# Attention of the first four tiles in the form of the later ones, with a set time for each step of the plan

## The chip, the cores and the metric

One core of a Trainium2 chip runs the whole program. The time is device microseconds of one execution, given as the median of three runs; the profile is of a fourth execution, taken by the hardware profiler, with its own time. The engines are TensorE (PE; its weight loads PEld), VectorE (DVE), ScalarE (ACT), GpSimd (POOL) and SyncE (SP), which issues all the transfers of this kernel on one queue.

## The reference

Chunked attention, then two pairs of dense layers on its output:

```python
# q, k, v: (4, 8, 768, 64); mem_k, mem_v: (4, 8, 8, 64); chunks of 32, 16 to the left, 8 to the right
for c in range(nc):
    q_c = q[:, :, c_start:c_end]
    k_full = np.concatenate([mem_k, k[:, :, l_start:r_end]], axis=2)
    v_full = np.concatenate([mem_v, v[:, :, l_start:r_end]], axis=2)
    scores = scale * np.matmul(q_c, k_full.transpose(0, 1, 3, 2))
    scores = scores - np.max(scores, axis=-1, keepdims=True)
    a = np.exp(scores)
    a = a / (np.sum(a, axis=-1, keepdims=True) + 1e-09)
    out[:, :, c_start:c_end] = np.matmul(a, v_full)
x = out as (3072, 512)
h = x @ w_in;  g = np.maximum(h, 0) + alpha * np.minimum(h, 0);  x = g @ w_out        # 512 -> 2048 -> 512
h = x @ w2_in; g = h * np.tanh(softplus(h));                     out = g @ w2_out
```

The weights come as 64-bit floats.

## The kernel before

The 3072 rows are 24 tiles of 128 rows (T); four tiles make a block of 512 rows. Each number is split into a high and a low part (`xh`, `xl`; `gh`, `gl`), and a product is three matmuls. The program is in stages: the attention of tiles 0 to 3; layer 1 over the blocks, into which the attention of the later tiles is woven two tiles at a time; the last blocks of layer 1 and then layer 2 in a form with seven products for eight.

Nothing runs in the order in which it is written. Every operation is given to a plan (`plan.add`) with an engine, an estimated duration and what it reads and writes. `Plan.run` derives due times backwards from the TensorE operations, whose own due time is `plan.now` at the moment of adding (a running sum of TensorE durations), plays the plan through with these estimates, and emits each engine's operations in the order that comes out. Before the first matmul of layer 1 the gaps that the plan sees on TensorE are filled with matmuls on a zero tile (`busy`).

Three kinds of steps make the attention of a tile: scores `s`, transposes `t` and values `v`; `first` lists them for the tiles 0 to 3. There are two forms:

- **The first four tiles** (`scores_of`, `turn_pe`, `values_of`). The queries of two heads lie in one wide tile (`qbd`) whose other halves GpSimd sets to zero and into which VectorE (ScalarE once) copies the loaded rows (`place`); a score matmul gives 64 x 64. The probabilities lie in wide rows padded with zeros, and 16 small transposes a tile turn them; the values lie on 96 partitions, and a value matmul contracts over these.
- **The later tiles** (`scores_late`, `turn_late`, `values_late`), two at a time. The queries are used as they are loaded, a score matmul gives 32 x 64 in one of two banks, one 128 x 128 transpose serves two heads, and the values lie on 2 x 64 partitions, so that a row needed by two chunks is loaded twice.

For the tiles in `WHOLE` (2 and 3) the exponential is one instruction after a subtraction on VectorE, with a sum behind it; for the others it is one instruction for each of eight groups, which gives the sum too.

A `gate` is a transfer of one element out of a tile. It can only be issued when the tile has landed (or been scaled by ScalarE), and it holds the queue until then, so that the loads behind it start later:

```python
add("sp", 0.001, lambda: nc.sync.dma_start(gated[:, n : n + 1], first() if first else b.t[0:1, 0:1]), [b], at=-1.0, not_before=when)
```

A weight is loaded as 64-bit words (`load_raw`, L320 for input weights, L325 for output weights), scaled by ScalarE (L339), put together by VectorE (L342, L345) and split (L356, L359). `evac` stores the output of layer 1 in `yd`; `reload1` loads a split output weight back (`wo<-w1o`, L418); `sent` loads a weight of layer 2 (`wo<-w2i`, L437).

Lines: scores L632, exponentials L650 (by group) and L660 (whole), transposes L868 and copies out of them L267, values L699, layer 1's first product L1087 and second L1136, rectifier L1106 and L1107, fillers L1684. In the later form: scores L755, transposes L892, values L821 and their loads L591 and L598.

Of the kernel before, what the change touches and what calls it, by code (L numbers as in the profile page):

```python
# [20 lines left out]
NEG = -1.0e30  # L21
# [169 lines left out]
def chunked_attention_moe_moe_kernel(  # L191
# [39 lines left out]
    WHOLE = (2, 3)  # L231
# [37 lines left out]
    def dma_(b):  # L269
        return max(0.45, b / (285e3 if not plan.now else 310e3 if 390 < plan.now < 700 else 265e3))  # L270
# [173 lines left out]
    spare = [(side, j) for j in range(NJ - 1, NJ - 7, -1) for side in "oi"]  # L444
# [10 lines left out]
    qbd = [own([P, 1024], f"qbd{i}") for i in range(2)] + [spare_slot() for _ in range(2, T0)]  # L455


    q_own, upper = ([Buf(lambda b=b, lo=lo: b.t[:, lo : lo + 512], [b]) for b in qbd[:2]] for lo in (0, 512))
    kring = ring(ac, [P, NP * KC], F32, "kt", 1)
    vring = ring(ac, [P, 2 * DM], F32, "vw", 1)  # L460
    q_rows = [spare_slot() for _ in range(T0 // 2)]
# [3 lines left out]
    s_bufs = [own([P, 1024], "s"), spare_slot()]  # L465
    a_bufs = [own([P, 1024], "aT"), spare_slot()]

    def wide_of(b):
        return b.t.rearrange("p (g w) -> p g w", w=P)

    for b in s_bufs:
        for cols in (slice(0, CH), slice(CH + SW, P)):
            add("pool", 0.6, lambda b=b, cols=cols: nc.gpsimd.memset(wide_of(b)[:, :, cols], 0.0), writes=[b])
    for b in qbd:
        for h in range(2):
            add(
                "pool", 0.6,
                lambda b=b, h=h: nc.gpsimd.memset(
                    b.t.rearrange("p (g h x) -> p g h x", g=2 * NP, h=2)[(1 - h) * 64 : (2 - h) * 64, :, h], 0.0
                ),  # L480
                writes=[(b, 2 + h)],
            )
    stats = ring(ac, [P, 3, 2 * NP], F32, "st", 3)
    stats2 = ring(ac, [P, 3, 4 * NP], F32, "su", 2)
# [3 lines left out]
    att_bufs = [*s_bufs[:1], *a_bufs[:1], *qbd[:2], *q_own, *upper]  # L488
    n_ps = [0]
# [16 lines left out]
    def load_qk(T):  # L506
        b, t = divmod(T, TPB)
        if T >= T0:
            load_qk_late(T)
            return  # L510
        kt = kv_spare[T][0] if T in kv_spare else kring.next()
        qt = qbd[T]

        def kview():
            return kt.t[:, : NP * KC].rearrange("p (a c) -> p a c", a=NP)

        def qview():
            return qt.t.rearrange("p (a e h x) -> p a e h x", a=NP, e=2, h=2)

        add("sp", dma_(P * NP * KC * 4), lambda: nc.sync.dma_start(kview(), kw[b, t]), writes=[kt])  # L520
        if T == 3:
            gate(kt, 12.7)

        row = q_rows[T // 2], T % 2

        def rows():
            return row[0].t[:, row[1] * 512 : (row[1] + 1) * 512]

        add("sp", dma_(P * 2048), lambda: nc.sync.dma_start(rows(), q[b, t].rearrange("h d a e x -> (h d) (a e x)")), writes=[row])
# [7 lines left out]
        kts[T], qs[T] = (kt, kview), (qt, qview)  # L537
        att_bufs.append(kt)

# [30 lines left out]
    def load_v(T):  # L570
        b, t = divmod(T, TPB)
        if T < T0:
            v = kv_spare[T][1] if T in kv_spare else vring.next()
# [5 lines left out]
            vws[T] = v, lambda: v.t[:W].rearrange("w (e h d) -> w e h d", e=2, h=H)  # L579
            att_bufs.append(v)  # L580
            return

        bufs = upper if T % 2 else [vring.next()]
        for e in range(2):
            half = slice(e * 64, (e + 1) * 64)
            rows = vw[b, 2 * t + e].rearrange("w h d -> w (h d)")
            if T % 2:
# [13 lines left out]
        if not T % 2:  # L601
            att_bufs.append(bufs[0])

        def value(half, c, h):
            x = (0 if T % 2 else c * DM) + h * D
            return bufs[c if T % 2 else 0].t[half, x : x + D]
# [3 lines left out]
    def scores_of(T):  # L610

        t = T % TPB
        (kt, kview), (qt, qview) = kts[T], qs[T]
        bk = att_bank(T, 6)
        sb = s_bufs[T % 2 if T < T0 else 0]

        def s():
            return wide_of(sb)[:, :, CH : CH + SW]

        st = stats.next()  # L620
        ss[T] = sb

        def ps():
            return bk.t.rearrange("p (g c) -> p g c", c=SW)


        def go():
            for e in range(2):
# [11 lines left out]
        def clip():  # L640
            if t == 0:
                nc.vector.memset(ps()[0:64, 0:NP, 0:16], NEG)
# [1257 lines left out]
```

## Time and profile before

| | |
|---|---|
| median of 3 runs | 1056.91 us (1055.81 to 1058.74) |
| the profiled execution | 1057.76 us, span 1056.0 us |
| TensorE busy | 1048.8 us (99%) |
| VectorE, ScalarE busy | 766.8 us (73%), 603.4 us (57%) |
| granted TensorE clock | 1.000 |
| transfers | 256.68 MB, mean 243 GB/s |

The span is from the first to the last instruction; the time of an execution has a little more around it. A busy TensorE is one with a matmul in flight. Times of the trace are us from the start of the span.

### The profile page before, as it was taken

Reading aid. Unit: us, or ns where it says so; the run is one execution under the profiler, and the core shown is the slowest. Engines: PE = TensorE matmul, PEld = TensorE weight load, DVE = VectorE, ACT = ScalarE, POOL = GpSimd, SP = SyncE. Lnnn points to the kernel's source line nnn. Section 1 sums busy time; section 2 is a strip of 40 time slices with the busy share of each in tenths; the row PEclk is TensorE's granted clock in tenths of the full one; section 3 lists DMA queues with packets and bytes.
Section 4 is the critical chain, followed back from the end, with each engine's and each line's share of the span. In section 5 each row is a group of like instructions: output and inputs, shape, how many; then the busy total and the mean of one; then the engine's idle time right before and its main releaser. Section 6 shows DMA issues by size and latency. Waiting matters only on the chain.

```text
span 1056.0 us, 22372 instructions
## 1 busy us (share of the span) xinstructions
PE 1048.8 (99%) x8235; PEld 904.2 (86%) x8235; DVE 766.8 (73%) x1621; ACT 603.4 (57%) x1496; POOL 6.8 (1%) x19
## 2 busy tenths in 40 slices
PE   9999999999999999999999999999999999999998
PEld 6888888888888888888878889999999999999998
DVE  7999578878987899887792246875476875475586
ACT  6888555565667456666674344654454654454453
POOL 2000000000000000000000000000000000000000
PEclk9999999999999999999999999999999999999999
DMA  8978776785888764556789977787887778778786
GB/s 265 311 243 250 246 280 203 249 289 183 272 265 261 242 183 121 173 170 198 251 284 314 314 257 233 223 263 250 263 271 251 224 244 253 225 242 252 232 260 211
DMA packets 136742, 256.68 MB, mean 243 GB/s; under 512 B 13882, under 2 KB 38970, under 8 KB 136634
## 3 DMA queue, kind: packets, MB, share of 16 engines
q1 hardware_dynamic: 136634, 255.26, 75.0%
q8 instruction: 65, 1.06, 0.4%
q14 instruction: 43, 0.35, 0.1%
HBM read 203.56 MB, written 51.64 MB: 242 GB/s over the span
## 4 chain that ended last, share of the span: by engine, by line
PE 97%; DMA 1%; ACT 0%; SPq 0%; DVE 0%; issue 0%; DVEq 0%; ACTq 0%
PE bank L1377 23%; PE bank L1245 22%; PE bank L1136 17%; PE bank L1087 16%; PE bank L1666 8%; PE bank L1570 7%; PE bank L821 2%; PE bank L755 1%; PE bank L1684 1%; DMA wo<-w1o 1%; DMA wo<-in_w_out_dram 0%; PE bank L632 0%; SPq L437 0%; PE bank L699 0%; PE bank L892 0%
## 5 line engine op out<-in xcount | busy, mean ns | idle before, releaser
L1245 PE MATMUL bank<-wi,wo 128*128 128x512 f32 x672 | 180.8, 393 | 0.0
L1087 PE MATMUL bank<-xh,wi 128*128 128x512 f32 (+1 forms) x528 | 171.1, 386 | 0.2 <-ACT rstrip L1107 0.2
L1136 PE MATMUL bank<-gh,wo 128*128 128x512 f32 x512 | 169.6, 392 | 0.0
L1245 PEld LDWEIGHTS bank<-wi,wo 128*128 128x128 f32 x672 | 121.5, 189 | 21.2
L1087 PEld LDWEIGHTS bank<-xh,wi 128*128 128x128 f32 x528 | 98.1, 188 | 20.3 <-ACT rstrip L1107 0.4
L1136 PEld LDWEIGHTS bank<-gh,wo 128*128 128x128 f32 x512 | 96.2, 188 | 20.3
L1087 PE MATMUL bank<-xl,wi 128*128 128x512 f32 (+1 forms) x264 | 101.2, 384 | 0.0
L1136 PE MATMUL bank<-gl,wo 128*128 128x512 f32 x256 | 99.8, 390 | 0.0
L1245 PE MATMUL bank<-wo,wo 128*128 128x512 f32 x336 | 93.1, 393 | 0.0
L1377 PE MATMUL bank<-wo,wi 128*128 128x256 f32 x588 | 80.4, 283 | 0.0
L1377 PEld LDWEIGHTS bank<-wo,wi 128*128 128x128 f32 x588 | 77.1, 191 | 3.0
L1377 PE MATMUL bank<-wo,wo 128*128 128x256 f32 x558 | 76.9, 283 | 0.0
L1377 PEld LDWEIGHTS bank<-wo,wo 128*128 128x128 f32 x558 | 73.8, 191 | 3.1
L1099 ACT CAST gh<-rstrip 128x512 fp32r<-128x512 f32 x64 | 40.8, 638 | 54.3 <-DVE rstrip L1110 37.7
L1245 PEld LDWEIGHTS bank<-wo,wo 128*128 128x128 f32 x336 | 60.8, 189 | 10.1
L1110 DVE SCALAR_TENSOR_TENSOR rstrip<-rstrip,nalpha 128x512 f32<-128x512 f32 x64 | 47.9, 749 | 20.0 <-ACT rstrip L1107 19.1
L1106 ACT ACTIVATE rstrip<-bank 128x512 f32<-128x512 f32 x64 | 39.6, 619 | 33.9 <-PE bank L1087 33.7
L1087 PEld LDWEIGHTS bank<-xl,wi 128*128 128x128 f32 x264 | 49.7, 188 | 9.3
L909 DVE STREAM_TRANSPOSE aT<-s 32x256 f32<-32x256 f32 x128 | 55.8, 436 | 2.3
L1100 DVE TENSOR_TENSOR gl<-rstrip,gh 128x512 fp32r<-128x512 f32 x64 | 43.9, 687 | 18.1 <-ACT gh L1099 17.8
L1136 PEld LDWEIGHTS bank<-gl,wo 128*128 128x128 f32 x256 | 48.1, 188 | 9.8
L774 ACT ACTIVATE s<-bank,su 128x64 f32<-128x64 f32 x160 | 49.1, 357 | 4.4 <-DVE su L791 4.4
(416 smaller groups left out, 1994.7 us busy)
## 6 DMA issues: line engine op xcount, KB each, us to landing
wo<-w2o SPq DMA_DIRECT2D x237, 256.0 KB, 3.3
wo<-w2i SPq DMA_DIRECT2D x168, 256.0 KB, 3.4
wo<-w1o SPq DMA_DIRECT2D x49, 512.0 KB, 4.1
w2o<-wo SPq DMA_DIRECT2D x57, 256.0 KB, 3.0
w2i<-wo SPq DMA_DIRECT2D x56, 256.0 KB, 3.4
wo<-in_w_out_dram SPq DMA_DIRECT2D x24, 512.0 KB, 7.1
wi<-in_w_in_dram SPq DMA_DIRECT2D x16, 512.0 KB, 8.6
w1o<-wo SPq DMA_DIRECT2D x16, 512.0 KB, 5.3
```

The source lines that it names most:

```text
L774: nc.scalar.activation(s()[:, i, z, g], ps(z)[:, i, g], AF.Exp, bias=st.t[:, 0, n : n + 1], scale=0.125, accum_out=st.t[:, 1, n : n + 1],)
L909: nc.vector.transpose(dst[:, :, m // 2, m % 2], src[:, :, keys])
L1087: nc.tensor.matmul(bk.t[:, lo:hi], a, b, start=kk == 0 and i == 0, stop=kk == KT - 1 and i == 2)
L1099: add("act", a_(n), lambda: nc.scalar.copy(g.t[0], src.t[0]), [src], [(g, "h")], at=at)
L1100: add("dve", d_(n), lambda: nc.vector.tensor_sub(g.t[1], src.t[0], g.t[0].bitcast(F32)), [src, (g, "h")], [(g, "l")], at=at)
L1106: add("act", a_(n) - 0.05, lambda: nc.scalar.activation(m.t[0], h.t[:, :n], AF.Relu, scale=-1.0), [h], [m], at=at)
L1110: lambda: nc.vector.scalar_tensor_tensor(r.t[0], m.t[0], nalpha[:, j : j + 1], r.t[0], ALU.mult, ALU.add),
L1136: nc.tensor.matmul(bk.t[:, :n], lt, rh, start=j == 0 and i == 0, stop=j == NJ - 1 and i == 2)
L1245: nc.tensor.matmul(bk.t, l, r, start=start and kk == n == 0, stop=kk == 1 and n == 2, skip_group_check=True,)
L1377: nc.tensor.matmul(bk.t[:, s * HB : (s + 1) * HB], g.t[:, zg * HB + s * P : zg * HB + (s + 1) * P], piece()[:, zw * HB : (zw + 1) * HB], s ...
L1570: nc.tensor.matmul(bk.t, l, r, start=start and kk == n == 0, stop=kk == 1 and n == 2, skip_group_check=True,)
L1666: nc.tensor.matmul(bk.t, lt, rh, start=first and i == 0, stop=last_ and i == 2)
```

## The change

Tiles 0 to 3 use the form of the later tiles: `scores_of`, `values_of` and `turn_pe` are gone, and `scores`, `values` and `turn` (the former `_late` ones) work on one tile (`count(T)` is 1) or two. The queries are no longer copied and nothing is set to zero; each of the four tiles has its own `s` and `aT`. The values of a tile are two transfers to 64 partitions each. `WHOLE` holds tile 3 alone. The banks of the first tiles come from a list. The plan's clock is set by hand for each step of the first tiles and to 18.94 after them, where it was the sum of TensorE's durations. The estimate for a transfer and the gates' earliest times are changed.

```diff
-    WHOLE = (2, 3)
+    WHOLE = (3,)
 ...
-        return max(0.45, b / (285e3 if not plan.now else 310e3 if 390 < plan.now < 700 else 265e3))
+        return max(0.45, b / (345e3 if plan.now < 3 else 310e3 if 390 < plan.now < 700 else 265e3))
 ...
-    for b in qbd:
-        for h in range(2):
-            add(
-                "pool", 0.6,
-                lambda b=b, h=h: nc.gpsimd.memset(
 ...
+    n_ps = [-1]
+    FIRST = (0, 1, 2, 4, 5, 6, 7, 0, 1, 2, 4, 1, 7, 0, 1, 6, 1, 2, 6, 0)
 
     def att_bank(T, late):
         n_ps[0] += 1
-        return bank((0, 1, 2, 4, 5, 6, 7)[n_ps[0] % 7] if T < T0 else late)
+        return bank(FIRST[n_ps[0]] if T < T0 else late)
 ...
         if T == 3:
-            gate(kt, 12.7)
-
-        row = q_rows[T // 2], T % 2
 ...
-        for h in range(2):
-
-            def place(eng, h=h):
-                half = slice(h * 64, (h + 1) * 64)
-                copy_on(eng, qview()[half, :, :, h], rows()[half].rearrange("p (a e x) -> p a e x", a=NP, e=2))
-
-            add(BOTH if T == 0 else "dve", 0.55, place if T == 0 else partial(place, "dve"), [row], [(qt, h)])
+            gate(kt, 10.5)
 ...
-            src = vw[b, 2 * t : 2 * t + 2].rearrange("e w h d -> w e (h d)")
-            view = lambda: v.t[:W].rearrange("w (e x) -> w e x", e=2)
-            add("sp", dma_(P * 3520), lambda: nc.sync.dma_start(view(), src), writes=[v])
-            if T in (0, 2):
-                gate(v, 14.7 if T == 0 else 0.0)
 ...
+        apart = T >= T0 and T % 2
+        bufs = [kv_spare[T][1]] if T in kv_spare else upper if apart else [vring.next()]
         for e in range(2):
             half = slice(e * 64, (e + 1) * 64)
 ...
+        if T in (0, 2):
+            gate(bufs[0], 12.5 if T == 0 else 0.0)
 ...
+    def count(T):
+        return 1 if T < T0 else 2
 ...
+            whole = [i for i in range(ni) if T + i in WHOLE]
+            for i in whole:
+                for z in range(2):
+                    add("dve", d_(256), partial(less, i, z), [(st, 0, z), bks[z]], [(sb, i, z)])
 ...
-    first = "s0 s1 t0 s2 t1 s3 v0 t2 v1 t3 v2 v3"
-    block_steps = [[(st[0], int(st[1:])) for st in first.split()]]
+    first = "s0@4.05 s1@5.49 s2@7.58 s3@10.46 t0@11.96 v0@12.50 t1@13.50 v1@13.75 t2@14.58 t3@17.00 v2@17.87 v3@18.80"
+    block_steps = [[(st[0], int(st[1]), float(st[3:])) for st in first.split()]]
 ...
-    for st in block_steps[0]:
+    for *st, plan.now in block_steps[0]:
         run_step(st)
+    plan.now = 18.94
```

Where the plan puts things now. First the SP queue near its start, before: the values of tiles 0 and 1 (the `in_vw_dram` loads), then weights, with gates between.

```order
L576 DMA vw_205<-in_vw_dram 96x2x512
L576 DMA wi_221<-in_vw_dram 96x2x512
L320 DMA wi_252<-in_w_in_dram 128x4x256
L502 DMA gated<-wo_176 1x1
L320 DMA wi_289<-in_w_in_dram 128x4x256
L502 DMA gated<-vw_205 1x1
L576 DMA wi_326<-in_vw_dram 96x2x512
L502 DMA gated<-wi_252 1x1
L576 DMA wi_356<-in_vw_dram 96x2x512
L502 DMA gated<-wi_289 1x1
L320 DMA wi_380<-in_w_in_dram 128x4x256
```

The same place now (`wi_149` holds tile 3's keys; x2 is two transfers):

```order
L563 DMA vw_200<-in_vw_dram 64x2x512 x2
L563 DMA wo_249<-in_vw_dram 64x2x512 x2
L485 DMA gated<-wi_149 1x1
L320 DMA wi_299<-in_w_in_dram 128x4x256
L485 DMA gated<-vw_200 1x1
L320 DMA wi_362<-in_w_in_dram 128x4x256
L563 DMA wo_380<-in_vw_dram 64x2x512 x2
L485 DMA gated<-wi_299 1x1
L563 DMA wo_429<-in_vw_dram 64x2x512 x2
L485 DMA gated<-wi_362 1x1
L320 DMA wi_453<-in_w_in_dram 128x4x256
```

The first weight has moved behind the gate on tile 3's keys, and every tile's values are two transfers. Ahead of this stretch, the small load of `alpha` has moved from sixth place to first. On TensorE the fillers between the first score step and the first matmul of layer 1 are 27 instead of 21.

Second, ScalarE after the exponentials of tiles 0 and 1, before (`s` and `wo_113` are then the scores of tiles 2 and 3, `aT` and `wi_302` the turned ones of 0 and 1; `wi_252` and `wi_289` are the first two weights; `xh` is a value step's output):

```order
L267 COPY aT<-bank_257 96x16x32
L267 COPY aT<-bank_268 96x16x32
L267 COPY wi_302<-bank_279 96x16x32
L660 ACTIVATE s<-s 128x8x64
L660 ACTIVATE wo_113<-wo_113 128x8x64
L339 ACTIVATE wi_252<-wi_252 128x512
L716 CAST xh_349<-bank_304 128x4x128
L716 CAST xh_349<-bank_330 128x4x128
L339 ACTIVATE wi_289<-wi_289 128x512
```

And now (`wo_314` and `wi_312` are the scores of tiles 2 and 3, `wi_299` and `wi_362` the first two weights):

```order
L624 ACTIVATE wo_314,su_243<-bank_203,su_243 128x64
L267 COPY aT<-bank_304 128x512
L624 ACTIVATE wo_314,su_243<-bank_203,su_243 128x64 x3
L624 ACTIVATE wo_314,su_243<-bank_208,su_243 128x64 x4
L636 ACTIVATE wi_312<-wi_312 128x512
L339 ACTIVATE wi_299<-wi_299 128x512
L711 CAST xh_421<-bank_325 128x4x64
L711 CAST xh_421<-bank_328 128x4x64
L711 CAST xh_421<-bank_388 128x4x64
L711 CAST xh_421<-bank_385 128x4x64
L339 ACTIVATE wi_362<-wi_362 128x512
```

Tile 2's exponentials are eight instructions in place of one, and the copy for tile 0 stands among them.

Third, the SP queue where layer 1 ends, before (`w1o` are reloads for layer 1, `w2i` loads for layer 2):

```order
L418 DMA wo_6209<-w1o 128x1024
L1179 DMA b_5139<-yd 128x512
L437 DMA wo_6113<-w2i 128x512
L1156 DMA yd<-rstrip 128x512
L437 DMA wo_6247<-w2i 128x512 x2
L418 DMA wo_6265<-w1o 128x1024
L437 DMA wo_6281<-w2i 128x512
```

The same place now:

```order
L418 DMA wo_6353<-w1o 128x1024
L1001 DMA yd<-rstrip 128x512
L418 DMA wo_6378<-w1o 128x1024
L437 DMA wo_6288<-w2i 128x512
L437 DMA wo_6400<-w2i 128x512
L418 DMA wo_6410<-w1o 128x1024
L437 DMA wo_6400<-w2i 128x512
```

The two loads for layer 2 that stood between the `yd` store and the next reload have moved behind that reload.

## Rows read from the trace of the kernel before

**Rows 1.** Waits of TensorE, whole run: who, for whom, us in total, times, longest.

```profile
PE bank L1666 <- DMA wo<-w1o: 0.7, 1, 0.7
PE bank L699 <- ACT aT L267: 0.6, 2, 0.4
PE bank L1666 <- DVE wi L1648: 0.3, 1, 0.3
...
PE bank L1087 <- ACT rstrip L1107: 0.2, 1, 0.2
```

**Rows 2.** Chain of waits, 20 to 40 us: start, us, what.

```profile
20.46 5.19 DMA wo<-in_w_out_dram
...
25.68 0.70 ACT wo L339
...
27.65 0.62 ACT wo L356
...
29.31 3.06 PE bank L1087 x12
```

**Rows 3.** Timeline of the SP queue, 0 to 36 us: start, us, what.

```profile
0.73 0.40 SPq L529 DMA_DIRECT2D wo<-in_q_dram  x1
...
6.76 0.39 SPq L320 DMA_DIRECT2D wi<-in_w_in_dram  x1
10.88 0.30 SPq L502 DMA_DIRECT2D gated<-wo  x1
...
17.45 0.23 SPq L502 DMA_DIRECT2D gated<-wi  x1
...
19.36 0.23 SPq L502 DMA_DIRECT2D gated<-wi  x1
```

**Rows 4.** Busy time by stretch; last columns: clock, DMA share, GB/s.

```profile
2.00:9.50 7.50, 7.22 (x79) 3.90 (x78) 3.83 (x9) 2.01 (x12) 5.46 (x12) 1.00 1.03 343
9.50:13.50 4.00, 4.00 (x73) 2.78 (x72) 2.93 (x11) 3.47 (x24) 0.00 (x0) 1.00 1.08 205
17.50:20.00 2.50, 2.50 (x46) 1.66 (x41) 2.50 (x9) 1.75 (x4) 0.00 (x0) 1.00 0.60 188
20.00:21.50 1.50, 1.10 (x33) 0.95 (x30) 1.50 (x4) 1.50 (x4) 0.00 (x0) 1.00 0.39 99
22.00:30.00 8.00, 7.77 (x89) 7.41 (x86) 7.00 (x12) 6.07 (x12) 0.00 (x0) 1.00 1.03 375
41.50:51.50 10.00, 10.00 (x46) 8.29 (x45) 8.76 (x19) 10.00 (x43) 0.00 (x0) 1.00 1.08 213
```

**Rows 5.** Timeline of TensorE: start, us, instruction, tiles, shape, count.

```profile
4.70 1.68 PE L632 MATMUL bank<-kt,qbd 128*64 128x64 f32 x32
...
8.31 1.25 PE L1684 MATMUL bank<-busy 128*128 128x512 bf16 x5
...
23.07 0.39 PE L1087 MATMUL bank<-xh,wi 128*128 128x256 f32 x1
...
53.00 1.03 PE L892 MATMUL bank<-ident,s 128*128 128x128 f32 x8
```

**Rows 6.** Chain of waits, two tiles' scores and values in the later form.

```profile
35.08 1.54 PE bank L755 x102
...
62.21 2.00 PE bank L821 x128
```

**Rows 7.** Timeline of ScalarE, first tiles: exponentials by group, whole exponential.

```profile
8.12 0.32 ACT L650 ACTIVATE s<-bank,st 128x64 f32<-128x64 f32 x1 [4.09 <-DVE st L677]
...
10.46 0.35 ACT L650 ACTIVATE wo<-bank,st 128x64 f32<-128x64 f32 x1
...
16.21 0.63 ACT L660 ACTIVATE wo<-wo 128x512 f32<-128x512 f32 x1
```

**Rows 8.** Timeline of the SP queue, 530 to 545 us.

```profile
536.73 2.79 SPq L437 DMA_DIRECT2D wo<-w2i  x2
539.62 0.38 SPq L418 DMA_DIRECT2D wo<-w1o  x1
```

More of the change, by code (lines that the diff above doesn't have):

```diff
@@ L441, in chunked_attention_moe_moe_kernel @@
     ac = att_pools.enter_context(tc.tile_pool(name="ac", bufs=1))
-    spare = [(side, j) for j in range(NJ - 1, NJ - 7, -1) for side in "oi"]
+    spare = [(side, j) for j in range(NJ - 1, NJ - 8, -1) for side in "oi"]
     def spare_slot():
@@ L731, in scores_late, with scores @@
-    def scores_late(T):
-        bks = [bank(6), bank(7)]
-        sb, st = s_bufs[0], stats2.next()
+    def count(T):
+        return 1 if T < T0 else 2
+    def scores(T):
+        ni = count(T)
+        bks = [att_bank(T, 6 + z) for z in range(2)]
+        sb, st = s_bufs[T if T < T0 else 0], stats2.next()
         ss[T] = sb
         def s():
-            return sb.t.rearrange("p (i z g k) -> p i z g k", i=2, z=2, k=SW)
+            return sb.t[:, : ni * 512].rearrange("p (i z g k) -> p i z g k", i=ni, z=2, k=SW)
@@ L739, in ps @@
         def ps(z):
-            return bks[z].t.rearrange("p (i g k) -> p i g k", i=2, k=SW)
+            return bks[z].t[:, : ni * 256].rearrange("p (i g k) -> p i g k", i=ni, k=SW)
         def stat(n):
-            return st.t[:, n, :].rearrange("p (i z g) -> p i z g", i=2, z=2)
+            return st.t[:, n, : ni * 2 * NP].rearrange("p (i z g) -> p i z g", i=ni, z=2)
         def go():
-            for i in range(2):
-                (_, keys), (_, qview) = kts[T + i], qs[T + i]
+            for i in range(ni):
+                (_, keys), (_, queries) = kts[T + i], qs[T + i]
@@ L762, in clip @@
         def clip(z):
-            for i in range(2):
+            for i in range(ni):
                 if (T + i) % TPB == 0:
@@ L795, in rest @@
                         add("act", 0.29, partial(exps, i, z, g), [(st, 0), bks[z]], [(sb, i, z, g), (st, 1, i, z, g)])
-            for i in range(2):
+            for i in range(ni):
                 ns = slice(i * 2 * NP, (i + 1) * 2 * NP)
@@ L804, in rest, with values @@
             att_bufs.append(st)
-        return go, [b for i in range(2) for b in kts[T + i][0] + qs[T + i][0]], bks, rest
-    def values_late(T):
+        return go, [b for i in range(ni) for b in kts[T + i][0] + qs[T + i][0]], bks, rest
+    def values(T):
         ab, aT = aTs.pop(T)
-        vs = [vws.pop(T + i) for i in range(2)]
-        bks = [bank(6), bank(7)]
+        ni = count(T)
+        vs = [vws.pop(T + i) for i in range(ni)]
+        bks = [att_bank(T, 6 + e) for e in range(2)]
         def go():
@@ L892, in turn, with back @@
                         nc.tensor.transpose(bks[i].t[:, p * P : (p + 1) * P], sb.t[:, cols], ident)
[L894 to L899 removed]
+            def back(i, eng="act"):
+                copy_on(eng, ab.t[:, i * 512 : (i + 1) * 512], bks[i].t)
+            add("pe", 0.55 * ni, by_pe, [sb] + behind(T), bks)
+            for i in range(ni):
+                add(BOTH if T < T0 else "act", a_(512), (lambda e, i=i: back(i, e)) if T < T0 else partial(back, i), [bks[i]], [(ab, i)])
             return
@@ L952, in run_step @@
                 load_v(T + 1)
[L953 removed]
+            T2 = T + count(T)
             if T2 < NTT:
```

243 lines of the change are left out of this document (64 added, 179 removed).

## Prediction

> **What bounds the kernel now.** I began with the table of engines: TensorE is busy for 1048.8 of 1056.0 us. The view of waits, TensorE alone, comes next: over the whole run its waits for others after the first attention steps are 0.7 us for a reloaded weight (`wo<-w1o`), 0.3 us for `wi` and 0.2 us for `rstrip`; inside those steps 0.6 us for `aT` [rows 1]. The reader is to see that from about 29 us to the end there is hardly one microsecond to win. So the change acts through one number: when the steady stream of layer-1 matmuls begins. After that it is a plain shift.
>
> The chain of waits between 20 and 30 us names what sets that moment [rows 2]. Layer 1's first four half-products start at 23.07 [rows 5], but the next product starts at 29.31, released by ScalarE's rectifier, and that stood in ScalarE's queue behind the scaling of the first output weight, which landed at 20.46 + 5.19 = 25.65. So the last thing to come is a transfer, not an attention step, although the attention steps run close beside it: the four half-products end just in time, with a wait of 0.2.
>
> Why does the weight land at 25.65? The SP queue says so [rows 3]: the loads are issued from 0.73, but 1x1 "gated" transfers hold the queue until an earlier tile has landed or has been scaled by ScalarE. The windows give the rates [rows 4]: queries and keys at 343 GB/s, the values of tiles 0 and 1 at 205 with the DMA engines fully busy (1.08), weights at 375, and two stretches where the gates leave the engines idle (188 GB/s at share 0.60, 99 at 0.39).
>
> **The change, part by part.** *Attention on TensorE.* The first score step took 1.68 [rows 5]; in the later form two tiles take 1.54, so one 0.77, and the values of two tiles 2.00, so 1.0 for one [rows 6]. The transposes of two tiles take 1.03, so 0.5 for one [rows 5]. But the new order also has 27 fillers instead of 21 between the first score step and the first product, at 1.25/5 = 0.25 each. TensorE runs in order, so a floor follows: 27 x 0.25 + 4 x (0.77 + 0.5 + 1.0) = 15.8 after the first score step. That step started at 4.70; its keys now have one small transfer (nalpha, 0.40 of issue) ahead, so 20.5 to 20.9 is the earliest first product, 2.2 to 2.6 before 23.07. No larger gain fits in front.
>
> *ScalarE and VectorE.* Tile 2 now takes its exponentials by groups. Eight groups cost 10.46 - 8.12 = 2.34, one whole exponential 0.63 [rows 7]: +1.7 on ScalarE. VectorE loses seven query copies and tile 2's subtraction and sum, GpSimd its zeroing. I cost all of this at nothing because a transfer covers it: ScalarE's exponentials can begin near 7.1 (5.1 for the score step, 0.77, then about 1.2 of VectorE), take 24 x 0.293 = 7.0, then a copy and tile 3's exponential, 1.2: the queue reaches the first weight's scaling near 15.3. That weight, issued only after the last keys have landed and queued behind four value transfers, lands near 16.7 by the ledger below: 0.73 + 0.4 + 7.1 + 4.9 (two tiles' values) + 1.4 (itself) = 14.5, and the latency of 2.2. The cover is 1.4; gone, ScalarE's 1.7 shows.
>
> *Transfers.* The values are now 64 partitions by two transfers a tile, with the overlapping rows loaded twice: 0.524 MB a tile instead of 0.393. The ledger, in MB and GB/s:
> before: queries and keys 2.43 at 343 = 7.1; values 1.57 at 205 = 7.7; four weight loads 2.10 at 375 = 5.6; sum 20.4. From the first issue at 0.73 to the landing at 25.65 there are 24.9; the remaining 4.5 are idle time, 2.5 x (1 - 188/375) + 1.5 x (1 - 99/375) = 2.35, and 2.2 of latency at both ends.
> after: the values are 2.10 MB. Their price from a row: the later tiles' values already have this form, and the stretch that holds them runs at 213 GB/s with engines fully busy (1.08) [rows 4]. That is 9.9, or 2.2 more. With the 0.4 of nalpha ahead, 2.6 more.
> How much of it fills the idle 2.35? All of it would leave +0.25; none, +2.6. The gates stay, and each waits for ScalarE to scale a weight that itself lands later, so the idle time partly moves along; I take half: 2.6 - 1.2 = **+1.4**.
> The row says that the 64-partition form is not faster per byte than the old one (213 against 205) and has a third more bytes. [...]
>
> *Later in the program.* Setting the clock of the plan to 18.94 after the attention steps shifts all later due times, and the order on SP and TensorE moves in places. The one that meets a wait is near 537: before, the reload that TensorE waited 0.7 for was issued at 539.62, behind two `wo<-w2i` loads that held the queue from 536.73 for 2.79 [rows 8]; now the reload stands directly behind the `yd` store, and those loads come after. That can return 0.7, and with the `wi` wait 1.0. The opposite end: the same shuffle makes new waits; the largest that TensorE has in the stream is 0.7, so two of these, +1.4. I take **-0.5**, most of the one wait that I can point at.
>
> **The sum.** Profiled execution 1057.76 (span 1056.0 and 1.8 around it): +1.4 - 0.5 = 1058.7. That execution lies 0.85 above the median of the three runs, 1056.91; on the median the sum gives **1057.8**. What a measurement can tell here is about 0.3%, 3.2 us, so this is no change.
>
> **The rivals.**
> *Nothing shows.* The gates' idle time swallows the additional bytes: +0.25 - 0.5, 1056.7. For it: 2.35 idle against 2.6 added. Against it: the loads in the idle stretch can't be issued before the gates open.
> *A gain.* If the two halves of a tile, in flight together, ran at the full 375, the values would take 5.6, 2.1 less than before; with 0.4 for nalpha the front gains 1.7, and TensorE's floor (2.2 to 2.6) allows it: 1056.9 - 1.7 - 0.5 = 1054.7. With the floor reached and all later waits gone it is 1053.4, just past the bound. Against it: 213 at a share of 1.08, where the engines were not idle.
> *Slower.* One mechanism, the gates: ScalarE's longer queue gets to the scaling of the first weight after it has landed, so the gate opens later, the values of tile 3 and the next two weights are issued later, and the idle time grows instead of being filled: 2.6 + 1.7 - 0.5 = +3.8, 1060.7. It decides from the point where ScalarE reaches that scaling more than 1.4 later than the 15.3 worked out above, for instance when its copy of tile 0's transposes, which stands ahead of seven of tile 2's exponentials, has to wait for TensorE. For it: ScalarE is in order, and the copies of both first value steps stand ahead of the second weight's scaling, for which the next gate waits. Against it: the cover of 1.4.
>
> **How the numbers follow.** The forecast (+0.3 to +2.6 in front) 0.58; nothing shows 0.15; gain 0.13; slower 0.14. Only half of the gain case passes 3.2 us: faster 0.07. The slower case passes it mostly, and a little of the forecast with new waits: slower 0.14; the rest, 0.79, is the same. The range takes in the gain's middle (1054.7) and the slower case's (1060.7), with a little for unknown new waits: 1054.7 to 1061.2. The likeliest case alone lies between 1056.5 and 1059.5.
>
> **What would show it.** Right: the product after the half-products starts at 30 to 31.5 instead of 29.31, the chain there again goes through the output weight's transfer; the stretch with the values of tiles 0 and 1 reads about 210 GB/s and lasts about 5 us; the first half-product starts at 23.5 to 25, released by the values of tile 3 (a wait on a DMA ahead of the last value step); ScalarE waits for the first weight near 16; the wait for `wo<-w1o` near 545 is gone. Wrong: value transfers well above 250 GB/s and a first product before 22; a wait of ScalarE's own making ahead of the first weight's scaling; or a new wait of more than 1.4 on TensorE after 32 us, since I have no term of that size there.

## The result

| | before | after |
|---|---|---|
| median of 6 runs | 1056.82 us (1055.81 to 1058.74) | 1066.26 us (1064.02 to 1069.40) |
| ratio, 95% interval | | 1.0089 (1.0071 to 1.0107) |
| profiled execution, span | 1057.76, 1056.0 us | 1066.94, 1065.2 us |
| first half-product, steady stream | 23.07, 29.31 us | 31.23, 38.26 us |
| from the stream's start to the end | 1026.7 us | 1026.9 us |

The change is slower by 9.4 us, where the forecast said no change, and outside its range. The last row says where: all of it is lost before the steady stream, in which layer 1's matmuls follow each other without a stop. The waits of TensorE over the whole run answer to [rows 1] (who, for whom, us in total, times, longest):

```profile
PE bank L605 <- issue: 2.7, 1, 2.7
PE bank L737 <- issue: 2.7, 2, 2.3
...
PE bank L932 <- ACT rstrip L952: 0.7, 1, 0.7
PE bank L1511 <- DMA wo<-w1o: 0.6, 1, 0.6
```

The two new lines name no releaser: "issue" is time in which TensorE waited for nothing that the profile shows; it is called a stand below. No such line of this size stands in the rows of before. The timeline of TensorE in the changed kernel shows where they fall, and answers to [rows 5]:

```profile
9.35 0.85 PE L605 MATMUL bank<-wi,wo 64*32 64x64 f32 x64
...
12.12 0.39 PE L605 MATMUL bank<-wi,wo 64*32 64x64 f32 x11 [0.94 <-DMA wo<-in_q_dram]
15.24 0.76 PE L605 MATMUL bank<-wi,wo 64*32 64x64 f32 x53 [2.73 <-issue]
16.34 1.06 PE L737 MATMUL bank<-ident,s 128*128 128x128 f32 x4 [0.33 <-issue]
17.19 1.91 PE L1529 MATMUL bank<-busy 128*128 128x512 bf16 x4
19.04 1.26 PE L690 MATMUL bank<-aT,vw 64*64 64x32 f32 x64
22.62 0.95 PE L737 MATMUL bank<-ident,wi 128*128 128x128 f32 x4 [2.32 <-issue]
...
29.19 1.14 PE L690 MATMUL bank<-wi,wo 64*64 64x32 f32 x64
30.14 1.11 PE L690 MATMUL bank<-wo,wo 64*64 64x32 f32 x64
31.23 0.47 PE L932 MATMUL bank<-xh,wi 128*128 128x256 f32 x1
...
38.26 0.50 PE L932 MATMUL bank<-xh,wi 128*128 128x512 f32 x1 [0.70 <-ACT rstrip L952]
```

The first stand lies inside a score step, after 11 of its 64 matmuls, and the same two tiles feed all 64: it isn't an operand that is missing. ScalarE (the same columns) is carried along, because the copy out of tile 0's transposes stands in its queue ahead of seven of tile 2's exponentials:

```profile
12.06 0.41 ACT L624 ACTIVATE wo<-bank,su 128x64 f32<-128x64 f32 x1
...
17.44 0.59 ACT L267 COPY aT<-bank 128x512 f32<-128x512 f32 x1 [4.88 <-PE bank L737]
...
20.48 0.69 ACT L339 ACTIVATE wi<-wi 128x512 f32<-128x512 f32 x1
```

So the first weight is scaled at 20.48, and on the SP queue the two gates that wait for such scalings open at 21.20 and 28.08 instead of 17.45 and 19.36 [rows 3], and the first output weight is issued at 29.20 instead of 20.46 [rows 2]:

```profile
11.17 0.32 SPq L485 DMA_DIRECT2D gated<-wi  x1
...
21.20 0.24 SPq L485 DMA_DIRECT2D gated<-wi  x1
...
28.08 0.24 SPq L485 DMA_DIRECT2D gated<-wi  x1
...
29.20 0.36 SPq L325 DMA_DIRECT2D wo<-in_w_out_dram  x1
```

The windows answer to [rows 4] (last columns: granted clock, DMA share, GB/s); the last two are laid on stretches behind the stands:

```profile
9.50:13.50 4.00, 1.91 (x78) 1.08 (x69) 1.76 (x6) 3.06 (x22) 0.00 (x0) 1.00 1.08 233
...
20.00:21.50 1.50, 0.30 (x23) 0.19 (x16) 0.00 (x0) 1.50 (x6) 0.00 (x0) 1.00 0.25 74
22.00:30.00 8.00, 7.00 (x141) 5.00 (x144) 6.11 (x16) 2.91 (x7) 0.00 (x0) 0.79 0.29 75
...
16.20:19.60 3.40, 3.26 (x36) 1.81 (x39) 2.07 (x7) 2.16 (x13) 0.00 (x0) 0.53 1.10 270
23.10:26.50 3.40, 3.18 (x66) 1.95 (x65) 2.86 (x9) 0.00 (x0) 0.00 (x0) 0.54 0.53 143
```

The transfers are idle for most of 20 to 30 us. And the granted clock, 1.00 in every stretch of [rows 4], falls behind each stand: TensorE, which had stood for 2.7 and 2.3 us, then runs at 0.53 and 0.54 in these two rows of 3.4 us, and four fillers take 1.91, where five took 1.25 in [rows 5].

**What comes in before the stands end.** The page lists a DMA queue of kind "instruction" (packets, MB, share):

```profile
q1 hardware_dynamic: 136954, 255.78, 75.0%
q8 instruction: 67, 1.10, 0.4%
```

67 packets are 1.10 MB, 16 KB each. They go with TensorE's program: the page of the kernel before has 65 of them for 16470 matmuls and weight loads, this one 67 for 16893, so 253 and 252 a packet. The DMA view of the tenth of a microsecond from 12.5 holds the start of one, and so does the tenth from 19.7:

```profile
q1 hardware_dynamic: 16, 0.02, 121.1%
q8 instruction: 1, 0.02, 82.8%
...
q8 instruction: 1, 0.02, 78.0%
```

By their records in the trace these two start at 12.57 and 19.73 and take 1.32 and 1.25 us, so they are in at 13.9 and 21.0, and TensorE goes on 1.35 and 1.64 us later. TensorE had issued 446 and 701 instructions by then, counted from the records (matmuls, weight loads and a few semaphore instructions). The two stands are 255 counted instructions apart, where a packet goes with 252 or 253, so TensorE may be waiting for a packet each time.

Three theories, then. **A, instructions:** the later form has twice as many TensorE instructions in a score or value step (64 matmul records a step for 32), so one packet's instructions are used up sooner than the next packet comes in over DMA engines that are full of loads (a share of 1.08 from 9.5 to 13.5). **B, bytes:** the values' transfers are what is late. **C, ScalarE and gates:** my slower rival; the stands are a symptom.

### The profile page after: what moved, and what is told of

Its sections match the earlier page's. It is cut to its first block, busy times and chain, and to the rows that moved or that the text cites. A ratio compares the mean times of both kernels' runs of the same rounds, so it can differ in the third digit from the quotient of the medians.

```text
span 1065.2 us, 22802 instructions
## 1 busy us (share of the span) xinstructions
PE 1050.1 (99%) x8443; PEld 903.3 (85%) x8450; DVE 765.7 (72%) x1624; ACT 604.1 (57%) x1509; POOL 0.9 (0%) x7
## 4 chain that ended last, share of the span: by engine, by line
PE 96%; DMA 2%; issue 1%; SPq 0%; ACT 0%; DVE 0%; DVEq 0%; ACTq 0%
PE bank L1222 22%; PE bank L1090 22%; PE bank L981 17%; PE bank L932 16%; PE bank L1511 8%; PE bank L1415 7%; PE bank L690 2%; PE bank L605 1%; DMA wo<-in_q_dram 1%; DMA wo<-w1o 1%; DMA wo<-in_w_out_dram 1%; DMA wo<-w2o 0%; PE bank L737 0%; PE bank L1529 0%; SPq L502 0%
```

## The experiments

Line numbers of a variant differ by a few from those of the kernel that it is made from. Each run was compared with runs of the kernel before on the same chip; the medians of those lie between 1057.05 and 1057.96. "Half-products" and "stream" are the first of each in the profiled execution, "count" is the number of TensorE instructions issued before, and the packets are those of the instruction queue. Where an expectation says when a packet was "asked for", that is my estimate: the moment at which TensorE passes the count 256 earlier (the step between the stands, counted below), which for the changed kernel's first packet (446 - 256 = 190) its trace has near 7.6. No record shows a request.

**Values later.** One gate more, ahead of the first two tiles' values.

```diff
+        if T == 0:
+            gate(kts[2][0][0], 7.5)
```

> The changed kernel with one 1x1 gate more: the loads of the first two tiles' values are held until tile 2's keys have landed (near 9 us). Nothing is removed. Theory A (instructions): TensorE's own instructions come in 16 KB packets over the same DMA engines (queue kind 'instruction'). The one whose packet starts at 12.57 was asked for near 7.7 and stood behind the value loads issued from 4.96 on; TensorE stands from 12.5 to 15.2 and again from 20.3 to 22.6 until such a packet is in. With the values issued after the request, the first packet should land by about 10.5, and the stand of 2.7 us in the fourth score step is gone or under 1; the half-products of layer 1 begin at 26 to 29 instead of 31.2, the time is 1060 to 1063. Theory B (bytes of the values): values that start 4 us later end later, so does all behind them: 1068 to 1070. Theory C (ScalarE's queue and the gates, TensorE's stands only a symptom): the stands stay, time 1066 to 1069.

Measured: 1062.23, ratio 1.0040 (1.0023 to 1.0057); half-products at 26.89, stream at 34.15. The stand at count 446 is gone, the one at 701 is shorter:

```profile
12.26 0.76 PE L607 MATMUL bank<-wi,wo 64*32 64x64 f32 x53 [0.34 <-issue]
13.18 0.60 PE L739 MATMUL bank<-ident,s 128*128 128x128 f32 x4 [0.16 <-DMA vw<-in_vw_dram]
13.61 1.03 PE L1531 MATMUL bank<-busy 128*128 128x512 bf16 x4
...
17.23 0.63 PE L739 MATMUL bank<-ident,wi 128*128 128x128 f32 x4 [1.39 <-issue]
```

The first packet starts at 9.84 instead of 12.57, and the four fillers take 1.03 again. As A has it, and against B and C: later loads made the kernel faster than the changed one.

**More instructions in the kernel before, without more columns.**

```diff
+    def filler(n):
+        for i in range(n):
+            c = slice(i * 512 // n, (i + 1) * 512 // n)
+            nc.tensor.matmul(idle.t[:, c], busy[:, :P], busy[:, c], start=True, stop=True)
...
+    plan.fill = lambda t: 0.44 if t < 6.8 else 0.22, partial(filler, 4)
```

> The kernel before with each filler matmul of 512 columns cut into four of 128: the same columns, 87 matmuls and 87 weight loads more. No attention step and no transfer differs. Theory A: TensorE reaches the end of its second block of instructions some 3 us earlier (near 13.6, at the first transposes), while the packet that starts at 14.46 can't be earlier, since the same loads are ahead of it: a stand of 2 to 3 us that the kernel before doesn't have, half-products at 25 to 26.5 instead of 23.07, time 1059 to 1060.5. Theories B and C: no change, 1056 to 1057.5.

Measured: 1059.66, 1.0023 (1.0012 to 1.0034), but no stand in the profiled execution (own time 1058.64, stream at 29.75). The packet did come earlier, at 11.37, which I had excluded. At the place that I had named, the first transposes, there is a wait:

```profile
14.02 0.71 PE L868 MATMUL bank<-ident,s 64*96 64x64 f32 x13 [0.74 <-DVE wo L666]
```

It ends 1.40 us behind the packet's end, as the stands do, but the profile names VectorE's L666, which had ended at 13.71. So at most 0.3 of it can be a wait for instructions, where I had given 2 to 3. The size of the loss agrees with A, its sign in the trace is too small; this run decides nothing.

**The count shifted.** The first eight fillers of the changed kernel in eight pieces each, 112 counted instructions more.

> The changed kernel with only its first eight fillers (ahead of the first score step) cut into eight pieces of 64 columns each: 56 matmuls and 56 weight loads more, all before 5 us, nothing else. Theory A: each end of a block comes 112 instructions earlier, so the requests go out earlier (near 5.7 instead of 7.7, ahead of most of the value loads): the stand in the fourth score step goes, a stand of up to 2 us can come in the third, the second stand shrinks: the half-products begin at 26 to 29, time 1060 to 1063; more instructions make it faster. Theories B and C: no change, 1065.5 to 1067.

Measured: 1065.24, 1.0070 (1.0050 to 1.0091): not measurably faster than the changed kernel, so the forecast gain failed. But the stands moved:

```profile
11.76 0.66 PE L605 MATMUL bank<-wi,wo 64*32 64x64 f32 x40 [1.79 <-issue]
...
18.46 1.02 PE L690 MATMUL bank<-aT,vw 64*64 64x32 f32 x56 [1.01 <-issue]
...
29.00 0.54 PE L690 MATMUL bank<-wo,wo 64*64 64x32 f32 x19 [2.06 <-issue]
```

They are in the third score step, the first and the fourth value step now, in other instructions on other data, and the counts are 447, 701 and 1211. A stand belongs to a count, not to a step. Together with one of 0.47 in the second value step they make 5.3 us, for 5.1 in the changed kernel, which fits a time that is hardly shorter.

**ScalarE relieved.** `WHOLE = (2, 3)` in the changed kernel.

> The changed kernel with tile 2's exponential whole again (WHOLE = 2 and 3), 1.7 us less on ScalarE. Theory A: TensorE has as many instructions as in the changed kernel and stands as long; half-products at 30 to 31.3, time 1065 to 1066.5. Theory C: ScalarE's queue is what delays the first weights and so the gates: the second gate on a weight opens 2 us or more earlier, time 1062 to 1063.5.

Measured: 1065.63, 1.0083 (1.0052 to 1.0114), stands of 3.02 and 1.00. C's gain isn't there.

**Half the instructions.** The changed kernel's form, transfers and gates, with two chunks in one matmul; it leaves out the second chunk's own windows in tiles 0 to 3.

```diff
-                            for c in range(2):
+                            for c in range(ni if ni == 2 else 1):
...
+                                    if ni == 1:
+                                        nc.tensor.matmul(
+                                            ps(z)[(h ^ z) * 64 : (h ^ z) * 64 + 64, i, 2 * a + e, :],
+                                            queries()[half, 2 * a + z, e],
...
```

> The changed kernel, with the score and value products of the first four tiles in half as many instructions: one matmul of 64 x 64 takes the queries of both chunks of 32 (against the first chunk's keys), and one value matmul of 64 columns both chunks (with the first chunk's values). What is left out: the second chunk's own key and value windows in tiles 0 to 3. Transfers, gates, ScalarE and VectorE are those of the changed kernel. Theory A (instruction packets): 64 matmuls and weight loads a step in place of 128, so the counts 446 and 701, at which every kernel with a stand has stood so far, are reached near the first and the last value steps, after the packets are in: no stand of over 1 us ahead of 20 us; half-products at 24 to 26.5, time 1058.5 to 1061. What is then left over the time of before is the value bytes' term. Theories B (value bytes) and C (ScalarE and gates): no change from the changed kernel, 1064.5 to 1067.

Measured: 1062.37, 1.0050 (1.0038 to 1.0062); half-products at 26.23, stream at 33.10. No stand ("issue") of over 0.4 us is left there; the same steps as above:

```profile
13.21 0.79 PE L605 MATMUL bank<-wi,wo 64*64 64x64 f32 x32 [0.41 <-DMA wo<-in_q_dram]
14.16 0.60 PE L753 MATMUL bank<-ident,s 128*128 128x128 f32 x4 [0.16 <-issue]
14.60 1.03 PE L1545 MATMUL bank<-busy 128*128 128x512 bf16 x4
15.56 0.69 PE L699 MATMUL bank<-aT,vw 64*64 64x64 f32 x32
```

Half the instructions take back 0.39% of 0.89%. Not all of that need be stands: a value step takes 0.69 here and 1.14 there, so up to 1.8 us in four steps may be TensorE's own work. The run was to take back more: 5 us remain that A doesn't explain.

**Twice the instructions in the kernel before.** Each score and value matmul cut into two of 32 columns.

> The kernel before, with each score and value matmul of the first four tiles cut into two of 32 columns: the same products, twice as many instructions (128 in place of 64 matmuls and weight loads a step). Nothing else differs. Theory A: count 446 is reached near 12.5 (fourth score step) and the packet asked for near 7.5 is not in before 13.8: a stand of 1 to 2.5 us there, another near the first value step; half-products at 24.5 to 27, time 1059.5 to 1063. Theories B and C: no change, 1056.5 to 1058.5.

Measured: 1065.61, 1.0092 (1.0063 to 1.0121), half-products at 30.86; but not by stands, the longest of which is 0.31. TensorE itself got slower:

```profile
4.50 2.12 PE L633 MATMUL bank<-kt,qbd 128*64 128x32 f32 x64
```

A later score step of the kernel before (the first one took 1.68, [rows 5]):

```profile
9.49 1.18 PE L632 MATMUL bank<-wo,wo 128*64 128x64 f32 x32
```

64 matmuls of 32 columns take 2.12, where 32 of 64 columns took 1.18. With eight such steps, 7.5 of the 8.2 us are TensorE's own work. It tests nothing of A: the first stand's count is reached only at 15.0, when the packet has been in since 13.59.

**Without the gates on the weights**, in the changed kernel and in the kernel before.

```diff
-        if item in w1_items[:2]:
-            gate(raw, 0.0, lambda: words()[1][0:1, 0:1].bitcast(F32))
```

> The changed kernel without the two gates that wait for ScalarE's scaling of the first two weights: tile 3's values, the third weight and the first output weight are issued 6 to 9 us earlier. Theory A: both stands of TensorE stay as they are (12.3 to 15.2, 20.1 to 22.5), half-products near 30 to 31, the stream begins when they end, 36.3 to 37.5 instead of 38.3; time 1064.5 to 1066. Theory C (the gates are what makes it late): half-products and output weight come with their transfers, stream at 32 to 33, time 1060 to 1061.5.

> The kernel before without the two gates on the first weights. Theory A: the gates also keep the queue short while TensorE's packets are asked for; without them the packet needed at count 701 (near 22) is asked for near 17 behind 1.5 MB of loads more and comes 3 to 4 us later than at 18.1: a stand of 0 to 2 us in the last value steps, time 1056.5 to 1059. If gates only cost idle time: the output weight comes 2 to 3 us earlier, but the half-products end at 29.1 anyway, so at most 0.2 to win: 1056.5 to 1057.5.

Measured: 1066.82, 1.0095 (1.0081 to 1.0109) for the changed kernel, with stands of 3.23 and 2.59. The output weight was issued at 22.18 instead of 29.20 and nothing came of it: the gates only passed on what TensorE had lost. For the kernel before 1058.58, 1.0005 (0.9994 to 1.0016), no change; yet a stand has appeared, at count 705, in the last value step:

```profile
22.44 1.04 PE L697 MATMUL bank<-wi,wi 96*64 96x64 f32 x28 [0.33 <-ACT wi L354]
24.53 0.34 PE L697 MATMUL bank<-wi,wi 96*64 96x64 f32 x4 [1.05 <-issue]
```

Its packet starts at 21.99, in the kernel before at 18.09. Only loads were moved there, so that more of them are in flight: the packet is later for these, in the old form too. In these runs idle time behind a gate was no loss.

**The first weight ahead of the late values.**

> The changed kernel with the gate on tile 2's keys ahead of the first two tiles' values (as in the run with late values) and the first weight's load ahead of that gate, as early as in the kernel before. Theory A with the value bytes: 0.5 MB stand ahead of the first instruction packet, so a stand of 0 to 1.3 us at count 446; the first weight is scaled when ScalarE gets to it, near 17 instead of 19.0, both weight gates open 2 us earlier, stream at 31.5 to 33.5 instead of 34.2; time 1059 to 1061.5. If only the value bytes counted (theory B), no better than the run with late values, 1062 to 1063.

Measured: 1062.49, 1.0056 (1.0041 to 1.0071). The stand at 446 is back with 2.85 us, the packet starts at 11.71. I had given 0 to 1.3: half a megabyte of weights ahead of the packet does what the values did, so it isn't the values' form that holds it.

**The forecast's own term.** The kernel before with one load of 32 partitions more for each tile's values.

```diff
+                nc.sync.dma_start(view(), src)
+                nc.sync.dma_start(room(), more)
```

> The kernel before, with one load more for each of the first four tiles' values: 32 more partitions of 4 KB, into rows that nobody reads, so that a tile's values are 0.524 MB in two transfers as in the changed kernel. Everything else as before. The forecast's transfer term: the stream starts +1.0 later (+1.4 less the 0.4 of the small load), bounds -0.1 to +2.2, time 1057.5 to 1059.7. If the gates pass it on in full and more (the slower rival's mechanism without ScalarE): +2.5 to +4, 1060 to 1061.5. Theory A adds nothing here unless a packet is late by over 1 us, the slack that the kernel before has at count 446.

Measured: 1058.28, 1.0013 (1.0002 to 1.0025): +1.2 by the medians, for a forecast of +1.0. The profiled execution, at 1056.91 the fastest of twelve, shows the stream at 29.64, +0.3.

**What else is left with half the instructions.** The gates away; the first weight's load moved back; both weights' loads moved back.

```diff
-            gate(kt, 10.5)
+            gate(kt, 12.7)
...
-            gate(bufs[0], 12.5 if T == 0 else 0.0)
+            gate(bufs[0], 14.7 if T == 0 else 0.0)
```

> The run with half as many instructions (which leaves out the second chunk's own windows in tiles 0 to 3), and the two gates on the first weights taken away as well. If what is left there (stream at 33.1 instead of 29.3) is idle time behind these gates: tile 3's values and the first output weight come 3 to 4 us earlier, half-products at 24 to 25, stream at 30.3 to 31.5, time 1059 to 1060.5. If it is the value bytes alone, the queue is as long as before and the time stays at 1062 to 1063.

> The run with half as many instructions (which leaves out the second chunk's own windows in tiles 0 to 3), and the first weight's load back ahead of the gate on tile 3's keys (the gate's earliest time 12.7 as in the kernel before instead of 10.5). If the moved weight is what is left: it is scaled near 17.5 and both weight gates open 1.5 to 2.5 us earlier, time 1059.5 to 1061. If the value bytes are: ScalarE waited only 0.6 for this weight, so the gain is 0.6 at most, 1061.8 to 1063.

> The run with half as many instructions (which leaves out the second chunk's own windows in tiles 0 to 3), with the first two weights' loads both back at their places of before: the first ahead of the gate on tile 3's keys, the second ahead of the gate on tile 0's values (earliest times 12.7 and 14.7 instead of 10.5 and 12.5). If the order of these loads is what the bytes leave: ScalarE scales the second weight near 19.5 instead of 21.3 to 21.7, the stream starts at 30 to 31, time 1058.5 to 1059.8, what the bytes alone cost. If not: as with the first weight alone, 1060.5 to 1061.5.

> The changed kernel with only these two places changed back, all instructions as in the changed kernel. If TensorE's stands set the time there (theory A): stands at counts 446 and 701 as before, half-products at 30 to 31.2, time 1064.5 to 1066.3. If the order of the loads were the main cause: 1062 to 1063.5.

Measured: without gates 1062.96, 1.0046 (1.0031 to 1.0060), nothing. The first weight 1061.11, 1.0034 (1.0020 to 1.0048), and both 1060.99, 1.0032 (1.0022 to 1.0041): at most 1.3 to 1.7 us for the first, with intervals that touch that of the half count, and nothing for the second; in both a stand at 446 is back (0.79 and 1.13). In the changed kernel the order gives nothing: 1067.89, 1.0095 (1.0076 to 1.0114), stands of 3.27 and 1.25.

**The form of the value transfers.** The kernel before with two transfers of 64 partitions a tile, the same bytes as with more bytes.

```diff
+                for n in (0, 64):
+                    seen = bass.AP(x0.tensor, x0.offset + n * DM, [[DM, 64], [W * DM, 2], [1, DM]])
+                    nc.sync.dma_start(v.t[n : n + 64].rearrange("w (e x) -> w e x", e=2), seen)
```

> The kernel before, with each of the first four tiles' values loaded in two transfers of 64 partitions x 4 KB (the last 32 partitions are rows that nobody reads): the bytes of the run with more bytes (1058.3), in the partitions of the changed kernel. If transfers to 64 partitions are what is left: slower than that run, first weight scaled 1 us later or more, time 1059.5 to 1061. If only bytes count: 1058 to 1058.8, as there.

Measured: 1060.70, 1.0032 (1.0022 to 1.0042), +3.2 by the medians. That is as much as remains in the run with both weights moved back (1.0032). The profiled execution took 1059.24 and shows less of it: the stream at 30.61, +1.3, and the first weight scaled at 17.17, for 17.13 in the run with more bytes, so the 1 us given for that did not come. Compared with the run with more bytes the windows show nearly the same rate, first that run, then this:

```profile
9.50:13.50 4.00, 4.00 (x72) 2.73 (x68) 2.93 (x8) 2.96 (x20) 0.00 (x0) 1.00 1.08 248
```

```profile
9.50:13.50 4.00, 4.00 (x73) 2.77 (x72) 2.98 (x11) 3.49 (x24) 0.00 (x0) 1.00 1.06 240
```

but the SP queue spends longer on issuing, and the first weight behind these values goes out at 8.22 instead of 7.28:

```profile
4.96 1.37 SPq L582 DMA_DIRECT2D vw<-in_vw_dram  x2
6.93 1.25 SPq L582 DMA_DIRECT2D wi<-in_vw_dram  x2
8.22 0.59 SPq L320 DMA_DIRECT2D wi<-in_w_in_dram  x1
```

Whether the 2 us between the two medians are the issuing, the partitions or something that only other executions have isn't settled by this: the four slowest of the nine, 1061.55 to 1063.25, have a granted clock of 0.996 or 0.997, where the profiled one has 1.000.

**128 partitions in two transfers, split by chunk.** In the last of the half-count runs, in the changed kernel, and with late values.

```diff
+            seen = bass.AP(r0.tensor, r0.offset + c * CH * DM, [[W * DM, 2], [DM, SW], [1, DM]])
+            nc.sync.dma_start(bufs[0].t[:, c * DM : (c + 1) * DM], seen)
```

> The run with half as many instructions (which leaves out the second chunk's own windows in tiles 0 to 3) and both weights at their old places, with a tile's two value transfers split by chunk instead of by half: 128 partitions x 2 KB each, same bytes, same packets of 2 KB. If transfers to 64 partitions are what is left: the first weight is scaled near 17 instead of 19.0, stream 1.5 to 3 us earlier, time 1058 to 1059.5. If not: 1060.5 to 1061.5.

> The changed kernel with only the value transfers of the first four tiles split by chunk (128 partitions x 2 KB) instead of by half. If they move faster, the queue ahead of TensorE's instruction packets is shorter too: the first packet starts by 11.8 instead of 12.57, the stands shrink by 1 us each, time 1062 to 1064.5. If the form doesn't matter: 1065 to 1067.

> The run with late values (gate on tile 2's keys ahead of them, 1062.2) with the value transfers split by chunk as well. If the form of the transfers is what is left there: ScalarE's wait of 2.0 for the first weight goes, time 1058.5 to 1060.5, still not faster than before because of its bytes and a stand of 1 us. If not: 1061.5 to 1063.

Measured: 1094.05, 1096.62 and 1097.06, ratios 1.0346 to 1.0373. They don't answer the question, since these transfers were far slower than the halves; the window of the second one while values are in flight:

```profile
11.00:21.00 10.00, 3.23 (x82) 1.88 (x81) 3.48 (x12) 4.72 (x27) 0.00 (x0) 0.80 0.14 51
```

51 GB/s at a share of 0.14, where the halves read 233 at 1.08 in the changed kernel's stretch of values. Why this form is so slow isn't shown. No version tried is faster than the kernel before.

## Why the prediction was wrong

The stands of 0.8 us and more, as counted from the traces (instructions of TensorE with a record before each; length by the timeline):

```
changed kernel            446: 2.73    701: 2.32
values later                           701: 1.39   1210: 1.13
first fillers cut         447: 1.79    701: 1.01   1211: 2.06
ScalarE relieved          446: 3.02    701: 1.00
no weight gates           446: 3.23    701: 2.59
late, first weight early  446: 2.85
old order, changed kernel 446: 3.27    701: 1.25
half count, first weight  449: 0.79
half count, both weights  447: 1.13
before, no gates                       705: 1.05
```

In each of these 17 stands an instruction packet had ended 1.2 to 1.6 us before TensorE went on. The counts differ by a few because some records of matmuls are missing: 221 weight loads and 218 matmuls stand before the first one of the changed kernel. With one matmul for each weight load they are 449, 705 and 1217 in all 17, the first, second and fourth rungs of a ladder with steps of 256. The traces of all 20 kernels agree, up to the fifth rung: the first TensorE instruction behind a rung never starts less than 1.23 us after the end of the packet with the rung's number (the 16 KB packets counted from the start of the span). So the stands are waits for these packets. The kernel before stands at this edge itself: it passes 449 at 16.95, and its packet had ended at 15.61. It had no slack of over 1 us there, as the expectation of the run with more bytes has it.

**The step that failed is the floor of TensorE**, "27 x 0.25 + 4 x (0.77 + 0.5 + 1.0) = 15.8 after the first score step". It adds up durations and takes it that an engine always has its next instruction; the doubling of instructions was in the sum at nothing, and the chance that a new wait of over 1.4 comes up on TensorE was left to a clause at the end ("I have no term of that size there", said of the time after 32 us, when the two came before). What the runs showed in its place: two stands of 2.73 and 2.32, the slower clock behind them (0.53 and 0.54 over 3.4 us), and a queue of ScalarE and SP that follows, so that the first half-product came at 31.23 and not from 20.5 to 20.9 on. The durations themselves held: the last two value steps took 2.04 (29.19 to 31.23), for 2.0. Taking half of the instructions away took back 0.39% of the 0.89%, 4.1 us by the ratios, with an uncertainty of some 2.

**The transfer term was mis-sized.** It was +1.4 in front, +1.0 without the small load, worked out from bytes. For the bytes that holds (+1.2 by the medians). In two transfers of 64 partitions the same bytes cost 2 us more, 3.2 in all, beyond the bound of +2.6, though the trace shows +1.3 of it. The sentence that failed is that the 64-partition form "is not faster per byte than the old one": the stretch of the values, which holds other loads too, read 240 GB/s with it in the kernel before and 233 in the changed one, for 205, and it cost more all the same. So the rate of that stretch is not what sets the price. Why two transfers of 64 partitions cost more than one of 96 and one of 32 isn't shown: the rates with these are 240 and 248.

**ScalarE at nothing, under a cover of 1.4**, failed as foreseen in the slower rival: its copy of tile 0's transposes waited 4.88 for TensorE, and the first weight was scaled at 20.48 instead of 15.3. But that rival's mechanism isn't the cause. Tile 2's exponentials were worth nothing measurable, and without the gates the time stayed. Its price, +3.8, was less than half of what happened, because it had no stand in it.

**Later, -0.5:** +0.2 by the spans behind the stream's start. The wait for `wi` is gone, the one for the reloaded `wo<-w1o` is still 0.6 (0.7 before), though the two loads ahead of it had moved.

**The signs.** The stream began at 38.26, not at 30 to 31.5; the half-products at 31.23, not at 23.5 to 25; the stretch with the values read 233 GB/s, for about 210; ScalarE never waited for the first weight. The nearest of the listed signs of error is a wait of ScalarE ahead of that scaling, 4.88, but it was one for TensorE and not of ScalarE's own making. (The gain with the floor reached and all later waits gone, 1056.9 - 2.6 - 1.0, is 1053.3, not 1053.4.) What held: the chain again goes through the output weight's transfer (5.43 from 29.20); behind the stream's start nothing matters, and the change is a plain shift of that moment.

Half the instructions 4.1, transfers 3.2 and the first weight's place 1.3 to 1.7 make 8.6 to 9.0 of 9.4. These were measured in different kernels and with uncertainties of 1 to 2 us each, the first holds shorter value steps too, and in the changed kernel the weight's place gave nothing: the split is an estimate and isn't shown. **Open:** whether the runs with more value bytes have waits for packets in executions that weren't profiled, since the kernel before has no slack at 449. What makes a packet late is open too. When TensorE's sequencer asks for one isn't in the trace; that it waits among the loads rests on the runs in which loads alone were moved (12.57 to 9.84 with values later, 18.09 to 21.99 without gates in the kernel before). And why cut fillers cost the kernel before 1.7 us stays open.

## What to carry to other kernels

Count instructions, not only their durations: where a form has more and smaller matmuls, and the DMA engines are full, as here at a share of 1.08, an engine can wait for its own program, here for 2.73 and 2.32 us, and the profile calls that "issue" and names nobody. To tell it apart, shift the count by harmless instructions: a wait for data stays with its step, a wait for instructions with its number (446 and 701 here, 447 and 701 in other steps with the first fillers cut). Loads that are held back behind a gate may keep a way open for such packets (without the gates the kernel before had one start at 21.99 instead of 18.09, and a stand of 1.05 came up), so idle DMA time isn't always to be filled.

## What the hardware showed that I had not expected

- Single stands of 0.8 to 3.3 us of TensorE at fixed counts of its instructions, 256 apart, each ending 1.2 to 1.6 us behind a 16 KB packet on a queue of kind "instruction".
- A matmul over 128 rows of 32 columns takes as long as one of 64: 2.12/64 = 33 ns and 1.18/32 = 37 ns; over 64 rows in the later form 64 of them with 64 columns follow each other every 0.85/64 = 13 ns.
- Two transfers of 128 partitions whose source runs over 2 x 64 rows go at 49 to 51 GB/s, at a DMA share of 0.13 to 0.14.
